# Retention attention before two feed-forward experts: attention in units of half a batch, with states packed

## The chip, the cores and the metric

One NeuronCore of a Trainium2 chip runs the whole program. The metric is device time in microseconds of one execution, a median over timed runs. In the profile, PE is TensorE's matmuls and PEld its weight loads, DVE is VectorE, ACT ScalarE, POOL GpSimd, and SP SyncE, from which all transfers are issued.

## The reference

A decayed attention without softmax feeds two feed-forward layers, all in float32:

```
q, k, v: 4 batches x 8 heads x 576 positions x 64
scores = (q @ k^T) / 8
scores *= gamma_h ** (i - j)  for i >= j, else 0     (gamma_h = 1 - 2**(-5-h))
x = scores @ v                                       -> 2304 tokens x 512
h = max(max(x @ w1, x @ w2), x @ w3)                 512 -> 768
x2 = h @ w_out                                       768 -> 512
out = (silu(x2 @ w_gate) * (x2 @ w_val)) @ w_out2    512 -> 1536 -> 512
```

## The kernel before

**The attention.** Positions are cut into chunks of 96, three chunks to a half-batch of 288 positions. Heads go in pairs, so that two heads of 64 fill 128 partitions. Within a chunk the scores are computed and masked by the decay; what earlier chunks contribute is carried in a 64 x 64 state per head. `halves` lists 32 units (batch, head pair, half), the half running fastest, so a batch is complete after eight units. `a_load` loads a whole batch's keys, queries and values of a head pair (six transfers for two units). `a_prep` transposes keys and queries of a unit on TensorE through an identity (line 149), copies the keys out on ScalarE (kt, 153) and scales the queries by the decay on VectorE (qg, 154); for a first half GpSimd scales the keys (ks, 144). `a_score` multiplies them (168), and VectorE applies the decay mask (pT, 170). `a_state` forms the products of keys and values (185), and VectorE folds them into the running state, one 64 x 64 operation for each head and chunk (191, 193). The states lie in `stz` as 128 x 128 blocks, one head in the upper left and one in the lower right, with zeros elsewhere. `a_value` multiplies states by queries (208) and values by scores (214) into one accumulator, which leaves as a high half in float32r (xh, ScalarE, 220) and the rest (xl, VectorE, 221).

**The first expert.** Weights come as float64; `conv_w` turns a block of 128 x 512 into a high and a low float32r half, with two operations on ScalarE (102, 103), three on VectorE (104 to 106), one more on ScalarE (107) and a subtraction (108), on GpSimd for the first expert's 18 blocks, on VectorE for the later ones. `f_slice` is one *slice*: one block of 128 of the 768 hidden columns, one of w1, w2, w3, one half-batch; 12 matmuls of 288 columns (258) into one of two PSUM buffers. It is evicted on ScalarE (262) for w1 and with a maximum on VectorE (264) for w2 and w3, and after w3 stored to memory (266). There are 8 x 18 = 144 slices.

**The order.** TensorE's instructions run in the order of the program text (`manual_schedule`); those of the other engines are ordered by a planner that simulates the program. The loop over units weaves the attention of unit n (values), n+1 (scores and state) and n+2 (transposes) with slices of the batch before, in four visits: transposes, slices, scores, slices, values, slices, state, slices (lines 291 to 309). Nine slices go to two units. In the first seven units the 18 blocks are converted instead. Behind the loop stand the slices of the last batch, with the conversion of the second set of weights (`c2`, into 26 buffers that take over the attention's memory) and the reloading of h (`h_split`). Then come the product with w_out (line 381) and the second expert (from line 392 on).

Of the kernel before, what the change touches and what calls it, by code (L numbers as in the profile page):

```python
# [30 lines left out]
F1 = DF1 // P  # L31
# [31 lines left out]
def retention_moe(ctx, tc, consts, q, k, v, w1, w2, w3, w_out, w_gate, w_val, w_out2, out):  # L63
    nc = tc.nc
    pe, act, dve, pool, sp = nc.tensor, nc.scalar, nc.vector, nc.gpsimd, nc.sync

    def f(ap):
        return ap.bitcast(F32)
# [18 lines left out]
    e_t = cst[:, O_E:NCONST]  # L87
# [24 lines left out]

    halves = [(b, pr, h) for b in range(B) for pr in range(NP) for h in range(2)]
    NU = len(halves)
    U = {}
    xs = {}
    stz = [att.tile([P, 2 * NC, 2, D], F32, name=f"stz{i}", tag=f"stz{i}", bufs=1) for i in range(2)]
    for t in stz:  # L120
        pool.memset(t, 0.0)

    def a_load(u):
        if u >= B * NP:
            return
        b, pr = divmod(u, NP)
        t = {}
        for nm, s in (("k", k), ("q", q), ("v", v)):
            t[nm] = att.tile([CK, 2 * NC, 2, D], F32, name=f"{nm}n", tag=f"{nm}n", bufs=3)
# [3 lines left out]
        U[u] = t  # L133

    def a_prep(n):

        if n >= NU:
            return
        b, pr, h = halves[n]
        u = U[n // 2]  # L140
        if h == 0:
            ks = att.tile([CK, 2 * NC, 2, D], F32, name="ks", tag="ks")
            sc = ks_t[:, pr].unsqueeze(1).unsqueeze(3).to_broadcast([CK, 2 * NC - 1, 2, D])
            pool.tensor_tensor(ks[:, 0:2 * NC - 1], u["k"][:, 0:2 * NC - 1], sc, ALU.mult)
            u["ks"] = ks
        tp = psa.tile([P, 2, 512], F32, name="tp", tag="tp")
        for x, nm in ((0, "k"), (1, "q")):
            for c in range(NC):
                pe.transpose(tp[:, x, c * CK:(c + 1) * CK],  # L149
                             u[nm][:, h * NC + c].rearrange("p h d -> p (h d)"), ident)  # L150
        kt = att.tile([P, C], F32, name="kt", tag="kt")
        qg = att.tile([P, NC, CK], F32, name="qg", tag="qg", bufs=3)
        act.activation(kt, tp[:, 0, 0:C], ACTF.Copy)
        dve.tensor_tensor(qg, tp[:, 1, 0:C].rearrange("p (c m) -> p c m", c=NC),
                          g_t[:, pr].unsqueeze(1).to_broadcast([P, NC, CK]), ALU.mult)
        u[h] = {"kt": kt, "qg": qg}

    def a_score(n):
        if n >= NU:
            return  # L160
        b, pr, h = halves[n]
        w = U[n // 2][h]
        s = psa.tile([CK, 2, 512], F32, name="s", tag="s")
        for c in range(NC):
            cs = slice(c * CK, (c + 1) * CK)
            for e in range(2):
                hd = slice(64 * e, 64 * e + 64)
                pe.matmul(s[:, e, cs], w["kt"][hd, cs], w["qg"][hd, c], start=True, stop=True)  # L168
# [3 lines left out]
        w["pT"] = pT  # L172

    def a_state(n):
        if n >= NU:
            return
        b, pr, h = halves[n]
        u = U[n // 2]
        st = stz[(n // 2) % 2]
        m = psa.tile([P, NC, D], F32, name="m_ps", tag="m_ps")  # L180
        cs = [c for c in range(NC) if h * NC + c < 2 * NC - 1]
        for c in cs:
            g = h * NC + c
            for e in range(2):
                pe.matmul(m[64 * e:64 * e + 64, c], u["ks"][:, g, e], u["v"][:, g, e], start=True, stop=True)  # L185
        for c in cs:
            g = h * NC + c
            for e in range(2):
                hd = slice(64 * e, 64 * e + 64)
                if g == 0:  # L190
                    dve.tensor_copy(st[hd, 1, e], m[hd, c])
                else:
                    dve.scalar_tensor_tensor(st[hd, g + 1, e], st[hd, g, e], e_t[hd, pr:pr + 1], m[hd, c],  # L193
                                             ALU.mult, ALU.add)

    def a_value(n):
        if n >= NU or n < 0:
            return
        b, pr, h = halves[n]
        u = U[n // 2]  # L200
        w = u[h]
        st = stz[(n // 2) % 2]
        o = psa.tile([P, C], F32, name="o_ps", tag="o_ps")
        first = True
        for c in range(NC):
            g = h * NC + c
            if g:
                pe.matmul(o[:, c * CK:(c + 1) * CK], st[:, g].rearrange("p e d -> p (e d)"), w["qg"][:, c],  # L208
                          start=first, stop=False, skip_group_check=True)
                first = False  # L210
        for c in range(NC):
            g = h * NC + c
            for e in range(2):
                pe.matmul(o[64 * e:64 * e + 64, c * CK:(c + 1) * CK], u["v"][:, g, e], w["pT"][:, e, c],  # L214
                          start=False, stop=True, skip_group_check=True)
        if h == 0:
            u["x"] = [ffn.tile([P, S], F32R, name=f"x{x}", tag=f"x{x}{pr}", bufs=2) for x in "hl"]
        xh, xl = u["x"]
        ts = slice(h * C, h * C + C)
        act.activation(xh[:, ts], o, ACTF.Copy)  # L220
        dve.tensor_tensor(xl[:, ts], o, f(xh[:, ts]), ALU.subtract)
        xs[(2 * b + h, pr)] = (xh[:, ts], xl[:, ts])
        if h == 1:
            U.pop(n // 2)
# [52 lines left out]
    a_load(0)  # L277
    win_load(0)
    a_load(1)
    win_load(1)  # L280
# [8 lines left out]
    a_load(2)  # L289
    a_score(0)  # L290
    for n in range(NU):
        if n % 8 == 0 and n:
            b = n // 8 - 1
            fq += [(2 * b + h, fi, wi) for fi in range(F1) for wi in range(3) for h in range(2)]
        if n % 2 == 0:
            a_load(n // 2 + 3)
        quota = (2, 1, 1, 1) if n % 2 else (1, 1, 1, 1)
        ncv = (3 if n % 2 else 2) if n < 7 else 0
        a_prep(n + 2)
        f_some(quota[0])  # L300
        for _ in range(ncv):
            win_conv(wc)
            wc += 1
        a_score(n + 1)
        f_some(quota[1])
        a_value(n)
        f_some(quota[2])
        a_state(n + 1)
        f_some(quota[3])
    while wc < len(win_units):  # L310
        win_conv(wc)
        wc += 1
    f_some(99)
    pe_order.__exit__(None, None, None)
    psa_cm.__exit__(None, None, None)
    att_cm.__exit__(None, None, None)
# [157 lines left out]
```

## Time and profile before

| | us |
|---|---|
| three runs | 936.71, 936.80, 938.08; median 936.8 |
| profiled execution | 936.91 |
| its span, first to last instruction | 935.1 |
| TensorE busy (PE) | 898.9, 96% |
| VectorE busy (DVE) | 431.6, 46% |
| ScalarE busy (ACT) | 262.9, 28% |
| GpSimd busy (POOL) | 163.7, 18% |
| mean DMA rate | 71 GB/s |

The shares are means over stages of different kinds. The page's row of busy tenths shows TensorE at 9 in nearly all of 40 slices of the span, but at 5 to 8 in the first four, and VectorE at 8 or 9 in the second to fourth. The rows further down are from the single stages.

### The profile page before, as it was taken

How to read it: one execution, taken by the hardware profiler on the slowest of the kernel's cores; microseconds unless marked ns; L12 is line 12 of the kernel's file. 1: busy time of each engine (PE TensorE's matmuls, PEld its weight loads, DVE VectorE, ACT ScalarE, POOL GpSimd, SP SyncE). 2: the span in 40 equal slices, each digit the busy share in tenths (PEclk: the TensorE clock that was granted, in tenths of full speed). 3: DMA queues.
4: the chain of work that ended last, by engine and by line, in shares of the span. 5: the costliest groups of instructions: out<-in, count | busy, mean ns of one | idle time of the engine just before them, and what ended most of it. 6: DMA issues, size and time to landing. Idle time of an engine off the chain costs nothing.

```text
span 935.1 us, 14209 instructions
## 1 busy us (share of the span) xinstructions
PE 898.9 (96%) x5832; PEld 786.4 (84%) x5832; DVE 431.6 (46%) x816; ACT 262.9 (28%) x512; POOL 163.7 (18%) x148
## 2 busy tenths in 40 slices
PE   5876999999999999999999999999999999999998
PEld 4756999999999998999988888888888888888886
DVE  4899543444344388111172173465257335333243
ACT  2555111111111175034363271142133123111111
POOL 3354000000000040044411111111112111111111
PEclk9998999999999999999999999999999999999999
DMA  9975522322210166123240040021012000000112
GB/s 221 230 189 159 126 66 52 77 59 58 65 33 20 46 200 201 39 65 90 76 121 15 1 120 15 1 87 49 1 45 91 1 1 1 1 0 1 46 69 89
DMA packets 98225, 66.06 MB, mean 71 GB/s; under 512 B 59632, under 2 KB 93424, under 8 KB 98160
## 3 DMA queue, kind: packets, MB, share of 16 engines
q1 hardware_dynamic: 98160, 65.15, 25.3%
q8 instruction: 46, 0.75, 0.3%
q14 instruction: 19, 0.16, 0.0%
HBM read 53.34 MB, written 11.80 MB: 70 GB/s over the span
## 4 chain that ended last, share of the span: by engine, by line
PE 84%; DVE 7%; DMA 3%; issue 2%; ACT 2%; POOL 1%; SPq 0%; POOLq 0%; DVEq 0%; ACTq 0%
PE ps L406 31%; PE ps L258 22%; PE ps L428 15%; PE ps L381 7%; DVE wz L105 2%; PE o_ps L214 2%; PE s L168 2%; PE o_ps L208 2%; PE tp L149 1%; DVE wz L104 1%; DVE wl L106 1%; PE m_ps L185 1%; DMA h_d<-hmax 1%; DMA w<-in_moe_w_gate_dram 1%; DVE stz L193 1%
## 5 line engine op out<-in xcount | busy, mean ns | idle before, releaser
L258 PE MATMUL ps<-xl,wh 128*128 128x288 f32 x576 | 181.4, 315 | 9.6 <-DVE hmax L264 7.2
L406 PE MATMUL ps<-x2l,wrh 128*128 128x512 f32 (+1 forms) x480 | 179.3, 374 | 0.8 <-DVE sg L414 0.8
L406 PE MATMUL ps<-x2h,wrl 128*128 128x512 f32 (+1 forms) x480 | 179.1, 373 | 0.0
L406 PE MATMUL ps<-x2h,wrh 128*128 128x512 f32 (+1 forms) x480 | 179.1, 373 | 0.0
L258 PE MATMUL ps<-xh,wlo 128*128 128x288 f32 x576 | 170.8, 297 | 0.0
L258 PE MATMUL ps<-xh,wh 128*128 128x288 f32 x576 | 170.5, 296 | 0.0
L417 POOL TENSOR_TENSOR gl<-gf,gh 128x512 fp32r<-128x512 f32 (+1 forms) x60 | 75.3, 1256 | 388.7 <-ACT gh L416 388.7
L258 PEld LDWEIGHTS ps<-xl,wh 128*128 128x128 f32 x576 | 109.3, 190 | 18.8 <-DVE hmax L264 9.0
L414 DVE TENSOR_TENSOR sg<-ps,sg 128x512 f32<-128x512 f32 (+1 forms) x60 | 38.2, 636 | 171.1 <-ACT sg L413 171.1
L258 PEld LDWEIGHTS ps<-xh,wlo 128*128 128x128 f32 x576 | 109.4, 190 | 0.0
L258 PEld LDWEIGHTS ps<-xh,wh 128*128 128x128 f32 x576 | 109.2, 190 | 0.0
L406 PEld LDWEIGHTS ps<-x2l,wrh 128*128 128x128 f32 x480 | 90.4, 188 | 19.7 <-DVE sg L414 1.6
L406 PEld LDWEIGHTS ps<-x2h,wrl 128*128 128x128 f32 x480 | 90.3, 188 | 17.8
L406 PEld LDWEIGHTS ps<-x2h,wrh 128*128 128x128 f32 x480 | 90.4, 188 | 17.7
L428 PE MATMUL ps<-wrh,gl 128*128 128x512 f32 x216 | 85.8, 397 | 0.4 <-POOL gl L417 0.4
L428 PE MATMUL ps<-wrl,gh 128*128 128x512 f32 x216 | 85.5, 396 | 0.0
L428 PE MATMUL ps<-wrh,gh 128*128 128x512 f32 x216 | 85.2, 394 | 0.0
L413 ACT ACTIVATE sg<-ps 128x512 f32<-128x512 f32 (+1 forms) x60 | 33.2, 554 | 166.6 <-PE ps L406 166.6
L264 DVE TENSOR_TENSOR hmax<-ps,hmax 128x288 f32<-128x288 f32 x96 | 43.8, 456 | 76.4 <-PE ps L258 71.9
L416 ACT ACTIVATE gh<-gf 128x512 fp32r<-128x512 f32 (+1 forms) x60 | 35.2, 586 | 121.3 <-DVE gf L415 121.3
L415 DVE TENSOR_TENSOR gf<-ps,sg 128x512 f32<-128x512 f32 (+1 forms) x60 | 38.2, 637 | 65.9 <-PE ps L406 64.8
L355 POOL TENSOR_TENSOR hl<-hf,hh 128x288 fp32r<-128x288 f32 x48 | 40.4, 860 | 143.3 <-ACT hh L354 142.3
(51 smaller groups left out, 1233.6 us busy)
## 6 DMA issues: line engine op xcount, KB each, us to landing
w<-in_moe_w_dram SPq DMA_DIRECT2D x18, 512.0 KB, 4.8
w<-in_moe_w_out_dram SPq DMA_DIRECT2D x18, 512.0 KB, 3.7
h_d<-hmax SPq DMA_DIRECT2D x48, 144.0 KB, 1.8
hf<-h_d SPq DMA_DIRECT2D x48, 144.0 KB, 2.2
w<-in_moe_w_gate_dram SPq DMA_DIRECT2D x12, 512.0 KB, 4.4
w<-in_moe_w_val_dram SPq DMA_DIRECT2D x12, 512.0 KB, 4.6
kn<-in_k_dram SPq DMA_DIRECT2D x32, 144.0 KB, 4.2
qn<-in_q_dram SPq DMA_DIRECT2D x32, 144.0 KB, 4.4
```

What stands on the lines that cost most here:

```text
L105: dve.scalar_tensor_tensor(z, u[:, :, 1], 0x80000000, z, ALU.bitwise_and, ALU.bitwise_or)
L258: pe.matmul(ps, l[:, ksl], r, start=n == 0, stop=n == 3 * KD - 1)
L264: dve.tensor_tensor(mx[hb], ps, mx[hb], ALU.max)
L355: pool.tensor_tensor(hl, hf, f(hh), ALU.subtract)
L381: pe.matmul(ps, l[:, es], r, start=n == 0, stop=n == 3 * F1 - 1)
L406: pe.matmul(ps[:, 0:tw], l[:, ksl], r, start=n == 0, stop=n == 3 * KD - 1)
L413: act.activation(sg[:, 0:tw], pr[0][:, 0:tw], ACTF.Sigmoid)
L414: dve.tensor_tensor(sg[:, 0:tw], pr[0][:, 0:tw], sg[:, 0:tw], ALU.mult)
L415: dve.tensor_tensor(gf[:, 0:tw], pr[1][:, 0:tw], sg[:, 0:tw], ALU.mult)
L416: act.activation(gh[:, 0:tw], gf[:, 0:tw], ACTF.Copy)
L417: pool.tensor_tensor(gl[:, 0:tw], gf[:, 0:tw], f(gh[:, 0:tw]), ALU.subtract)
L428: pe.matmul(ps, l[:, sl], r, start=n == 0, stop=n == 3 * GRP - 1)
```

## The change

Units are now (batch, half, head pair), the pair running fastest, so that a half-batch is complete after four units. Each unit has its own loads, four units ahead. A loop pass makes one visit of values n, state n+1 and scores n+1, then slices, then the preparation of n+2, then slices. From unit 8 on (`PT`) keys and queries are loaded once more in pieces of 32 partitions with runs of 32 numbers (8 more transfers a unit, the ones for natural queries left out), and VectorE transposes them in blocks of 32 x 32. The state of both heads is one packed 128 x 64 operation; two ScalarE copies a unit spread it into zeroed tiles, and the product with the queries is made for each head with 64 columns. Conversions are due one a unit in units 1 to 3 and three a unit in 4 to 8; slices start at unit 4 with three a unit, and five a unit from unit 9 on. The last half-batch's 18 slices stand behind the loop.

```diff
-    halves = [(b, pr, h) for b in range(B) for pr in range(NP) for h in range(2)]
+    PT = 8
+    units = [(b, h, pr) for b in range(B) for h in range(2) for pr in range(NP)]
...
+            if nm == "q" and n >= PT:
+                continue
+            u[nm] = att.tile([CK, NC, 2, D], F32, name=f"{nm}n", tag=f"{nm}n", bufs=4)
             for e in range(2):
-                sp.dma_start(out=t[nm][:, :, e, :],
-                             in_=s[b, 2 * pr + e].rearrange("(a p) d -> p a d", p=CK))
+                sp.dma_start(out=u[nm][:, :, e, :],
+                             in_=s[b, 2 * pr + e, c0:c0 + C].rearrange("(a p) d -> p a d", p=CK))
+        if n >= PT:
+            u["t"] = att.tile([P, 2, C // 32, 32], F32, name="qk", tag="qk", bufs=3)
+            for i, s in enumerate((k, q)):
+                for e in range(2):
+                    for x in range(2):
+                        g = 64 * e + 32 * x
+                        sp.dma_start(out=u["t"][g:g + 32, i],
+                                     in_=s[b, 2 * pr + e, c0:c0 + C, 32 * x:32 * x + 32].rearrange("(a p) d -> p a d", p=32))
...
+            qt = att.tile([P, C], F32, name="qt", tag="qt", bufs=2)
+            dve.transpose(kt.rearrange("p (a d) -> p a d", d=32), u["t"][:, 0])
+            dve.transpose(qt.rearrange("p (a d) -> p a d", d=32), u["t"][:, 1])
+            dve.tensor_tensor(qg, qt.rearrange("p (c m) -> p c m", c=NC), g, ALU.mult)
...
+        for c in range(nk):
             g = h * NC + c
+            if g == 0:
+                act.activation(st[:, 1], m[:, c], ACTF.Copy)
+            else:
+                dve.scalar_tensor_tensor(st[:, g + 1], st[:, g], e_t[:, pr:pr + 1], m[:, c], ALU.mult, ALU.add)
+        z = stz[n % 3]
+        for e in range(2):
+            hd = slice(64 * e, 64 * e + 64)
+            act.activation(z[hd, 1 - h:NC, e], st[hd, h * NC + 1 - h:(h + 1) * NC], ACTF.Copy)
...
+                if c or h:
+                    pe.matmul(oc, z[:, c, e], u["qg"][:, c], start=c == 1 - h, stop=False, skip_group_check=True)
...
     a_prep(0)
-    win_conv(wc)
-    wc += 1
     a_state(0)
+    a_score(0)
     a_prep(1)
...
+        if n % NP == 0 and n:
+            fq += [(n // NP - 1, fi, wi) for fi in range(F1) for wi in range(3)]
+        a_load(n + 4)
+        a_value(n)
+        a_state(n + 1)
+        a_score(n + 1)
+        quota, ncv = ((2, 3) if n >= 9 else (1, 2)), 0
+        if 1 <= n < 4:
+            ncv = 1
+        elif 4 <= n < 9:
+            ncv = 3
+        for _ in range(min(ncv, len(win_units) - wc)):
             win_conv(wc)
             wc += 1
+        f_some(quota[0])
+        a_prep(n + 2)
         f_some(quota[1])
...
-    fq += [(2 * (B - 1) + h, fi, wi) for fi in range(F1) for wi in range(3) for h in range(2)]
+    fq += [(NHB - 1, fi, wi) for fi in range(F1) for wi in range(3)]
     for i in range(F1):
         c2()
         h_split(0, i)
-        f_some(6)
+        f_some(3)
     f_some(99)
```

## Rows read from the trace of the kernel before

**Rows 1.** Windows: busy us (x instructions) of each engine, clock, DMA share, GB/s.
```profile
6.50:95.50 89.00, 67.83 (x516) 57.50 (x516) 78.78 (x145) 43.72 (x82) 35.08 (x25) 0.96 0.86 203
120.00:300.00 180.00, 180.00 (x1696) 168.00 (x1693) 74.04 (x188) 25.05 (x61) 10.01 (x8) 1.00 0.21 56
```

**Rows 2.** Groups by line, VectorE, 6.5 to 95.5 us: count, busy us, mean ns, idle before.
```profile
L105 DVE SCALAR_TENSOR_TENSOR wz<-w,wz 128x512 uint32<-128x512 uint32 x20 | 20.3, 1013 | 0.5
L104 DVE TENSOR_SCALAR wz<-wz 128x512 uint32<-128x512 uint32 x21 | 16.3, 777 | 0.7 <-ACT wz L102 0.5
L106 DVE CUSTOM_DVE_ANT_0 wl<-wz,wl 128x1024 uint16<-128x1024 uint16 x20 | 15.7, 787 | 0.7
L193 DVE SCALAR_TENSOR_TENSOR stz<-stz,cst,m_ps 64x64 f32<-64x64 f32 x40 | 11.1, 278 | 1.0
L170 DVE TENSOR_TENSOR pT<-s,cst 96x576 f32<-96x576 f32 x10 | 7.5, 751 | 0.8 <-PE s L168 0.7
L154 DVE TENSOR_TENSOR qg<-tp,cst 128x288 f32<-128x288 f32 x12 | 5.5, 455 | 9.9 <-ACT kt L153 9.6
```

**Rows 3.** Chain of work that ended last: start us, us, what.
```profile
371.45 24.13 PE ps L258 x180
395.58 7.17 PE ps L381 x54
```

**Rows 4.** TensorE in order of time, 201 to 223 us: start us, us, line.
```profile
201.15 0.75 PE L168 MATMUL s<-qg,kt 64*96 64x96 f32 x12
201.84 0.40 PE L258 MATMUL ps<-xl,wh 128*128 128x288 f32 x1
...
203.53 0.80 PE L208 MATMUL o_ps<-qg,stz 128*128 128x96 f32 x6
204.27 0.72 PE L214 MATMUL o_ps<-pT,vn 96*64 96x96 f32 x12
204.91 0.40 PE L258 MATMUL ps<-xl,wh 128*128 128x288 f32 x1
...
206.69 0.57 PE L185 MATMUL m_ps<-vn,ks 96*64 96x64 f32 x12
207.19 0.40 PE L258 MATMUL ps<-xl,wh 128*128 128x288 f32 x1
...
208.89 0.41 PE L149 MATMUL tp<-cst,kn 96*128 96x96 f32 x3
...
209.33 0.38 PE L258 MATMUL ps<-xl,wh 128*128 128x288 f32 x1
...
211.09 0.75 PE L168 MATMUL s<-qg,kt 64*96 64x96 f32 x12
...
222.29 0.75 PE L168 MATMUL s<-qg,kt 64*96 64x96 f32 x12
```

**Rows 5.** TensorE in order of time, 19.5 to 26 us, one unit of the front.
```profile
19.81 0.74 PE L149 MATMUL tp<-cst,kn 96*128 96x96 f32 x3
...
20.96 1.28 PE L168 MATMUL s<-qg,kt 64*96 64x96 f32 x12
22.17 1.59 PE L208 MATMUL o_ps<-qg,stz 128*128 128x96 f32 x6
23.69 1.23 PE L214 MATMUL o_ps<-pT,vn 96*64 96x96 f32 x12
24.71 0.85 PE L185 MATMUL m_ps<-vn,ks 96*64 96x64 f32 x12
25.49 0.74 PE L149 MATMUL tp<-cst,kn 96*128 96x96 f32 x3
```

**Rows 6.** Groups by line, 329.8 to 395.4 us: the first of three matmul groups.
```profile
L258 PE MATMUL ps<-xl,wh 128*128 128x288 f32 x152 | 46.1, 303 | 2.3 <-DVE hmax L264 1.4 <-ACT hmax L262 0.7
```

**Rows 7.** Line 131's transfers, ns to issue min/median/max: 100 to 330, 0 to 40 us.
```profile
L131 SPq DMA_DIRECT2D qn<-in_q_dram x14: 457/478/501, 114.3 to 241.6; - x14
...
L131 SPq DMA_DIRECT2D vn<-in_v_dram x10: 313/780/1642, 3.3 to 39.4; - x10
```

More of the change, by code (lines that the diff above doesn't have):

```diff
@@ L111, in cols, with a_load @@
         return w[:, c0:c0 + P].rearrange("(a p) n -> p a n", p=P)
-    halves = [(b, pr, h) for b in range(B) for pr in range(NP) for h in range(2)]
-    NU = len(halves)
+    PT = 8
+    units = [(b, h, pr) for b in range(B) for h in range(2) for pr in range(NP)]
+    NU = len(units)
     U = {}
     xs = {}
-    stz = [att.tile([P, 2 * NC, 2, D], F32, name=f"stz{i}", tag=f"stz{i}", bufs=1) for i in range(2)]
+    states = {}
+    stz = [att.tile([P, NC, 2, D], F32, name=f"stz{i}", tag=f"stz{i}", bufs=1) for i in range(3)]
     for t in stz:
         pool.memset(t, 0.0)
-    def a_load(u):
-        if u >= B * NP:
+    def a_load(n):
+        if n >= NU:
             return
-        b, pr = divmod(u, NP)
-        t = {}
+        b, h, pr = units[n]
+        c0 = h * C
+        u = {}
         for nm, s in (("k", k), ("q", q), ("v", v)):
-            t[nm] = att.tile([CK, 2 * NC, 2, D], F32, name=f"{nm}n", tag=f"{nm}n", bufs=3)
+            if nm == "q" and n >= PT:
+                continue
+            u[nm] = att.tile([CK, NC, 2, D], F32, name=f"{nm}n", tag=f"{nm}n", bufs=4)
             for e in range(2):
-                sp.dma_start(out=t[nm][:, :, e, :],
-                             in_=s[b, 2 * pr + e].rearrange("(a p) d -> p a d", p=CK))
-        U[u] = t
+                sp.dma_start(out=u[nm][:, :, e, :],
[8 more added lines that the diff above has]
+                                     in_=s[b, 2 * pr + e, c0:c0 + C, 32 * x:32 * x + 32].rearrange("(a p) d -> p a d", p=32))
+        U[n] = u
     def a_prep(n):
@@ L138, in a_prep @@
             return
[L139 to L150, printed above, removed]
@@ L151, in a_prep @@
-        kt = att.tile([P, C], F32, name="kt", tag="kt")
-        qg = att.tile([P, NC, CK], F32, name="qg", tag="qg", bufs=3)
[L153 to L156, printed above, removed]
+        b, h, pr = units[n]
+        u = U[n]
+        nk = NC - h
+        u["ks"] = att.tile([CK, NC, 2, D], F32, name="ks", tag="ks", bufs=3)
@@ new lines, in a_prep @@
+        sc = ks_t[:, pr].unsqueeze(1).unsqueeze(3).to_broadcast([CK, nk, 2, D])
+        pool.tensor_tensor(u["ks"][:, 0:nk], u["k"][:, 0:nk], sc, ALU.mult)
+        kt = att.tile([P, C], F32, name="kt", tag="kt", bufs=2)
+        qg = att.tile([P, NC, CK], F32, name="qg", tag="qg", bufs=3)
+        g = g_t[:, pr].unsqueeze(1).to_broadcast([P, NC, CK])
+        if n < PT:
+            tp = psa.tile([P, 2, 512], F32, name="tp", tag="tp")
+            for x, nm in ((0, "k"), (1, "q")):
+                for c in range(NC):
+                    pe.transpose(tp[:, x, c * CK:(c + 1) * CK],
+                                 u[nm][:, c].rearrange("p h d -> p (h d)"), ident)
+            act.activation(kt, tp[:, 0, 0:C], ACTF.Copy)
+            dve.tensor_tensor(qg, tp[:, 1, 0:C].rearrange("p (c m) -> p c m", c=NC), g, ALU.mult)
+        else:
[3 more added lines that the diff above has]
+            dve.tensor_tensor(qg, qt.rearrange("p (c m) -> p c m", c=NC), g, ALU.mult)
@@ L160, in a_score @@
             return
-        b, pr, h = halves[n]
-        w = U[n // 2][h]
+        b, h, pr = units[n]
+        u = U[n]
         s = psa.tile([CK, 2, 512], F32, name="s", tag="s")
@@ L167, in a_score @@
                 hd = slice(64 * e, 64 * e + 64)
-                pe.matmul(s[:, e, cs], w["kt"][hd, cs], w["qg"][hd, c], start=True, stop=True)
+                pe.matmul(s[:, e, cs], u["kt"][hd, cs], u["qg"][hd, c], start=True, stop=True)
         pT = att.tile([CK, 2, NC, CK], F32, name="pT", tag="pT")
@@ L176, in a_state @@
             return
-        b, pr, h = halves[n]
-        u = U[n // 2]
-        st = stz[(n // 2) % 2]
+        b, h, pr = units[n]
+        u = U[n]
+        nk = NC - h
         m = psa.tile([P, NC, D], F32, name="m_ps", tag="m_ps")
-        cs = [c for c in range(NC) if h * NC + c < 2 * NC - 1]
-        for c in cs:
-            g = h * NC + c
+        for c in range(nk):
+            for e in range(2):
+                pe.matmul(m[64 * e:64 * e + 64, c], u["ks"][:, c, e], u["v"][:, c, e], start=True, stop=True)
@@ new lines, in a_state @@
+        if h == 0:
+            st = states[(b, pr)] = att.tile([P, 2 * NC, D], F32, name="st", tag=f"st{pr}")
+        else:
+            st = states.pop((b, pr))
+        for c in range(nk):
+            g = h * NC + c
+            if g == 0:
+                act.activation(st[:, 1], m[:, c], ACTF.Copy)
+            else:
+                dve.scalar_tensor_tensor(st[:, g + 1], st[:, g], e_t[:, pr:pr + 1], m[:, c], ALU.mult, ALU.add)
+        z = stz[n % 3]
+        for e in range(2):
+            hd = slice(64 * e, 64 * e + 64)
+            act.activation(z[hd, 1 - h:NC, e], st[hd, h * NC + 1 - h:(h + 1) * NC], ACTF.Copy)
@@ L184, in a_state, with a_value @@
+    def a_value(n):
+        b, h, pr = units[n]
+        u = U.pop(n)
+        z = stz[n % 3]
+        o = psa.tile([P, C], F32, name="o_ps", tag="o_ps")
+        for c in range(NC):
             for e in range(2):
-                pe.matmul(m[64 * e:64 * e + 64, c], u["ks"][:, g, e], u["v"][:, g, e], start=True, stop=True)
-        for c in cs:
-            g = h * NC + c
+                oc = o[64 * e:64 * e + 64, c * CK:(c + 1) * CK]
+                if c or h:
+                    pe.matmul(oc, z[:, c, e], u["qg"][:, c], start=c == 1 - h, stop=False, skip_group_check=True)
+        for c in range(NC):
@@ L188, in a_state @@
             for e in range(2):
[L189 to L214, printed above, removed]
-                          start=False, stop=True, skip_group_check=True)
[L216 to L224, printed above, removed]
@@ L227, in retention_moe @@
+                pe.matmul(o[64 * e:64 * e + 64, c * CK:(c + 1) * CK], u["v"][:, c, e], u["pT"][:, e, c],
+                          start=False, stop=True, skip_group_check=True)
+        xh, xl = [ffn.tile([P, C], F32R, name=f"x{x}", tag=f"x{x}{pr}", bufs=3) for x in "hl"]
+        act.activation(xh, o, ACTF.Copy)
+        dve.tensor_tensor(xl, o, f(xh), ALU.subtract)
+        xs[(2 * b + h, pr)] = (xh, xl)
     w_in = {}
@@ L277, in retention_moe @@
     a_load(0)
+    a_load(1)
     win_load(0)
-    a_load(1)
-    win_load(1)
+    a_load(2)
+    a_load(3)
     wc = 0
```

24 lines of the change are left out of this document (2 added, 22 removed).

## The prediction

> **What bounds the kernel now.** I read the windows by stage first, then the groups by line in the front, then TensorE's instructions in order of time. Up to 95.5 us VectorE sets the pace: it is busy 78.8 of 89.0 us (88.5%) while TensorE has gaps [rows 1]. What fills it is the conversion of the first expert's 18 weight blocks, 1.01 + 0.78 + 0.79 = 2.58 us of VectorE each, beside the attention's own operations [rows 2]. From 120 to 300 us TensorE is busy 180 of 180 us and VectorE 74 [rows 1]: there only TensorE's own work counts. The chain shows 15 slices in a row (180 matmuls, 12 a slice) in 24.13 us, 1.61 us a slice, and the second product (line 381) begins at 395.58 us [rows 3]. All after that point is untouched by the diff, so the sum is for the time of that point. The profiled execution took 936.91 us (span 935.1 and 1.8 around it), the median of the three timed runs is 936.8: no correction.
>
> **One unit in the steady part, before.** From score to score the first unit takes 211.09 - 201.15 = 9.94 us with four slices, the next 222.29 - 211.09 = 11.20 with five [rows 4]. Nine slices at 1.60 are 14.4, so attention costs (21.14 - 14.4)/2 = 3.37 us a unit. Inside the first unit the attention's own instructions are score 0.69, states times queries 0.74, values 0.64, state 0.50, transposes 0.44: 3.01. The rest, 9.94 - 6.40 - 3.01 = 0.53, is what four visits cost in starting and ending among slices: 0.13 each.
>
> **One unit after, from unit 9 on** (no transposes on TensorE, one visit, five slices behind it). Values 0.64, score 0.69, state 0.50 stay. The states' product was six matmuls of 128 columns; it becomes four or six of 64 columns for each half, in pairs on the two column halves. The trace has no such matmul with 128 rows. The nearest is the value product, whose halves lie on the column halves too: 12 in 0.64, 0.053 each [rows 4]. At that pace four to six are 0.21 to 0.32, mean 0.27. The other bound is that the pair doesn't overlap: 0.74/6 = 0.123 each, mean 0.62. I take 0.27, since the 96-row pairs differ only in rows. For entering and leaving I take 0.25: one visit is 0.13, and the visit now holds one more change of shape, from state to score.
> The trace can be counted in two ways here. By visits it is 0.13; the Trainium skill, "TensorEngine Tiling (Array Packing)", Key Properties, says that a change of tiling mode (not of tile) drains TensorE. Before, a unit has six such changes (into and out of scores, values and state; 0.53/6 = 0.09), after it three (slices to values, state to scores, scores to slices), 0.27 by that count. By the one the sum is 3 us lower than with 0.25, by the other 0.5 us higher.
> So a unit's attention is 0.64 + 0.69 + 0.50 + 0.27 + 0.25 = 2.35 us instead of 3.37, and its period with five slices 10.35 us.
>
> **The front.** Half-batches now come complete after four units instead of after eight units (a whole batch), so slices start at unit 4. TensorE's early pace is slower: the same score takes 22.17 - 20.96 = 1.21 us, values 1.02, state 0.78, transposes 1.15 [rows 5], against 0.69, 0.64, 0.50, 0.44 later, although the granted clock of the whole stretch is 0.96 in the mean [rows 1]. With 0.7 for the states' product a unit takes 4.9 us there. The first loads are half as large; I put the start of unit 0's values at 10 us, and unit 4 at 10 + 4 x 4.9 = 30 us. Until then only three conversions are due.
> From unit 4 to 8 three conversions are due per unit and VectorE binds again. Its work until all 18 blocks are converted: conversions 18 x 2.58 = 46.4; queries 11 x 0.455 = 5.0; scores 10 x 0.751 = 7.5; low halves of the output 9 x 0.455 = 4.1; states 20 x 0.278 = 5.6 (one operation on 128 x 64 for two on 64 x 64, of the same length by my choice, and the first of a first half goes to ScalarE); slices 10 x 0.455 = 4.5; six new transposes 2.7: 75.8 us [rows 2]. From 7 us on, at the 88.5% of before, that ends at 93. But unit 9's slices need only the first 15 blocks and then three more in turn: 3 x 2.58/0.885 = 8.7 us less, 84, and I take 86 for the start of unit 9 (by units: three conversions 7.7, attention 2.4 and slices 0.9 are 11.0 of VectorE's time a unit, and five of them from 30 on end at 85).
>
> **From unit 9 to line 381.** 15 of 144 slices are done. In the loop 111 remain: 177.6 us. Attention 23 x 2.35 less the missing last state and score, 52.9. Behind the loop 18 slices, 28.8. Before, the last 38 slices took 65.6 us against 60.8 at 1.60; the 4.8 are waits for evictions behind the next conversions [rows 6], which are all still there: I keep 4.8. Sum 264: line 381 starts at 350, 45 us earlier.
>
> **What I cost at nothing.** *VectorE in the steady part*: the new 32 x 32 transposes of 128 x 288 are not in the trace. I take 0.455 (same shape from PSUM); below nothing isn't possible, since they replace no VectorE work, and above I take 1.01 (the slowest 512-column row). A unit's VectorE work is then 3 x 0.455 + 0.751 + 0.455 + 0.56 + 1.5 = 4.6, at most 5.7, of 10.35 us. If this cover fails, an eviction waits behind the two transposes and the scaling (1.4, at most 2.5 us) and TensorE with it, having two accumulators: rival 2. *ScalarE* gains two small copies a unit and has 25 of 180 us in use [rows 1]; their path, state to copy to next visit, has five slices (8 us) of room. *POOL*: the same scaling of keys in smaller pieces. *SyncE and DMA*: a unit from 8 on issues 12 loads where two units shared 6, and its keys are loaded twice. At 0.478 us an issue [rows 7] that is 5.7, with 5/3 stores 6.4 of 10.35 us. Runs of 128 bytes double the pieces per unit; if each costs what one of 256 does, the DMA share of 0.21 [rows 1] becomes 0.4. Loads are four units ahead. The 18 blocks' loads are the same ones. *After the last values* 21 slices (34 us) cover the first six second-set conversions, which line 381 needs, as 38 did before.
>
> **Rivals.**
> 1. *Slow pace between 30 and 86 us.* TensorE has gaps there, and the same instructions are 1.75 times as long in the front (1.21/0.69). A unit would be 3 x 2.8 + 4.9 (3.75 from unit 6 on) = about 12.6 instead of 11.2: +7, end 899. For it: the granted clock of the stretch up to 95.5 us is 0.96 in the mean, so it fell to its lower level, 1.2 GHz, for a while [rows 1]. Against: slices come each few us.
> 2. *Evictions late in the steady part.* VectorE's work lies in one bunch around one visit, and a hmax eviction has 1.6 us. At 0.6 us a unit: +14, end 905; at 1.0, 914. For it: rows 6 show just such waits when VectorE is full. Against: it is full at 45% only.
> 3. *The unit doesn't shrink as said*: 64-column pairs one after another (+0.35) and shape changes dearer (+0.2): 23 x 0.55 = 13, end 904.
> 4. *Slower: SyncE's issue.* The loads of units 8 and on become the bound. Early loads took up to 1.64 us to issue, with a median of 0.78 [rows 7]. At 1.05 each a unit takes 12 x 1.05 + 0.6 = 13.2 us; 23 units are 304, plus 33.6 behind them and 86: line 381 at 423, end 965. It is slower than before from (395.6 - 86 - 33.6)/23 = 12.0 us a unit, 0.95 an issue. For it: the loads' halved runs and twice the issues. Against: 0.48 an issue where DMA isn't full. The Trainium skill, "DMA: Bandwidth & Descriptors", Specifications, wants transfers of 512 bytes for line rate, which speaks for this rival; no row here shows runs of 128.
> 5. *Better*: conversions pulled into the idle front, unit 9 at 76: end 881.
>
> **How the numbers follow.** Forecast 936.9 - 45.3 = 891.6, 891. Chances: forecast 0.45 (own range 884 to 898), rival 1 0.14, 2 0.17, 3 0.08, 4 0.05, 5 0.10, no change in sum 0.01. The range is 873 to 913: below, rival 5 with visits at 0.13 (878) and without the 4.8 of the last slices; above, rival 2 at its 914. Within 0.2%, 1.9 us, is about what a measurement can tell from no change: 0.01; faster 0.94, slower 0.05.
>
> **What would show it.** In the changed profile: slices from about 33 us; 15 done near 86; periods of 10.3 us with one visit; 12 values 0.64 and states' pairs 0.27; no gap of TensorE over 0.2 us between 100 and 310 us; line 381 near 350, and from there to the end of the span 539.5 us as before. It is wrong if TensorE waits for qk loads or for hmax in the steady part, or if unit 9 starts after 100 us.

## The result, and the profile after

The changed kernel takes 902.64 us (median of 4 runs, 902.10 to 904.41), the kernel before 936.75 on the same chip: ratio 0.9641, 95% interval 0.9619 to 0.9662. The forecast was 891 with 873 to 913: the direction and the range hold, and 11 us of the forecast gain did not come. The profiled execution took 902.46 us, 900.7 of them span.

Windows of the changed kernel by stage (busy us and instructions of TensorE, its weight loads, VectorE, ScalarE, POOL; granted clock; DMA share; GB/s). The first and the fourth answer to [rows 1]:

```profile
6.50:95.50 89.00, 66.61 (x648) 60.05 (x649) 66.37 (x125) 47.15 (x102) 34.44 (x31) 0.83 0.84 191
10.53:40.98 30.45, 19.38 (x197) 16.70 (x196) 16.29 (x33) 12.61 (x31) 10.00 (x10) 0.73 0.80 185
40.98:95.37 54.39, 43.23 (x417) 40.15 (x417) 48.28 (x88) 33.29 (x68) 23.34 (x19) 0.87 0.86 195
120.00:300.00 180.00, 180.00 (x1848) 174.14 (x1848) 76.11 (x183) 33.25 (x92) 12.06 (x17) 1.00 0.35 76
24.30:51.60 27.30, 18.00 (x152) 16.03 (x153) 19.23 (x36) 14.19 (x30) 8.83 (x8) 0.50 0.84 190
```

The second row is units 0 to 3. VectorE, which was busy 88.5% of the whole front before, has work for 16.3 of 30.5 us there, and TensorE for 19.4: no engine is the bound, and TensorE is idle for 11.1 us. The third row is units 4 to 8: VectorE 88.8%. The fourth is the steady part, TensorE without a pause.

TensorE of the changed kernel in order of time, one visit of the steady part, the counterpart of [rows 4], and the first instruction of the second product, the counterpart of [rows 3]:

```profile
202.41 0.29 PE L269 MATMUL ps<-xh,wh 128*128 128x288 f32 x1
202.64 0.55 PE L227 MATMUL o_ps<-qg,stz 128*64 128x96 f32 x8
203.02 0.67 PE L230 MATMUL o_ps<-pT,vn 96*64 96x96 f32 x12
203.52 0.40 PE L202 MATMUL m_ps<-vn,ks 96*64 96x64 f32 x8
203.85 0.75 PE L186 MATMUL s<-qg,kt 64*96 64x96 f32 x12
204.53 0.40 PE L269 MATMUL ps<-xl,wh 128*128 128x288 f32 x1
204.77 0.29 PE L269 MATMUL ps<-xh,wlo 128*128 128x288 f32 x1
...
359.26 0.30 PE L385 MATMUL ps<-hl,wrh 128*128 128x288 f32 x1
```

The line numbers have moved: slices 258 to 269, second product 381 to 385, and so on. From one start to the next the states' product takes 0.38 (0.55 where there are 12 records in place of 8), the values 0.50, the state 0.33 (or 0.45), the scores 0.68. Line 385 starts at 359.3, where 350 was forecast, and 541.4 us follow it, 539.5 before.

The starts of the units' value visits tell where the 11 us were lost (TensorE in order of time, us; the forecast's row is worked out from its terms, unit 31 with 98 slices after unit 11's):

| unit | 0 | 1 | 2 | 3 | 4 | 9 | 10 | 11 | 31 | line 385 |
|---|---|---|---|---|---|---|---|---|---|---|
| forecast | 10 | 14.9 | 19.8 | 24.7 | 30 | 86 | 96.4 | 106.7 | 310.5 | 350 |
| measured | 10.5 | 17.0 | 21.4 | 33.4 | 41.0 | 95.4 | 109.2 | 121.4 | 321.4 | 359.3 |

The loss arises in two places: units 2 and 3 (11 us late by unit 4), and units 9 and 10 (13.8 and 12.2 us for a period of 10.3, 5.3 us in all). What happens in unit 2 is seen with all engines in one order of time:

```profile
20.69 0.47 SPq L93 DMA_DIRECT2D w<-in_moe_w_dram  x1
21.44 0.55 PE L227 MATMUL o_ps<-qg,stz 128*64 128x96 f32 x8
24.79 0.66 ACT L102 ACTIVATE wz<-w 128x512 f32<-128x512 f32 x1 [3.89 <-DMA w<-in_moe_w_dram]
25.47 0.43 DVE L104 TENSOR_SCALAR wz<-wz 128x512 uint32<-128x512 uint32 x1 [5.00 <-ACT wz L102]
25.81 0.75 DVE L188 TENSOR_TENSOR pT<-s,cst 96x576 f32<-96x576 f32 x1
25.90 0.40 ACT L167 ACTIVATE kt<-tp 128x288 f32<-128x288 f32 x1
26.61 0.91 PE L230 MATMUL o_ps<-pT,vn 96*64 96x96 f32 x8 [4.62 <-DVE pT L188]
```

Read from below: TensorE waits 4.62 us for the masked scores `pT`. VectorE had their input, but the operation ahead of it in its queue was a step of a weight's conversion (line 104), which waited 5.00 us for ScalarE's step (line 102), and this waited 3.89 us for a transfer that SyncE had issued only at 20.69: 34 loads of keys, queries and values of units 0 to 5 stood ahead of it, and SyncE had issued one transfer every 0.55 us from 0.73 on. The copy `kt` stood behind line 102 in ScalarE's queue in the same way. Neither engine was at work: an operation that waits for a transfer blocked those behind it. Two more such waits follow, ahead of units 3 and 4:

```profile
33.36 1.23 PE L227 MATMUL o_ps<-qg,stz 128*64 128x96 f32 x8 [2.52 <-ACT stz L216]
39.21 0.48 DVE L172 STREAM_TRANSPOSE qt<-qk 128x288 f32<-128x288 f32 x1 [2.65 <-DMA qk<-in_q_dram]
40.98 1.44 PE L227 MATMUL o_ps<-qg,stz 128*64 128x96 f32 x11 [1.84 <-ACT stz L216]
```

At 33.36 TensorE waits for the states' copy (line 216), which stood behind a conversion that waited 1.40 us for its weight. At 40.98 it waits for the same copy of the next unit; that one waited for VectorE, whose head of queue was the transpose of a small load of queries. So the small loads already held up the front here, beside the weights.

At 24.3, while TensorE waited, its granted clock fell to 0.50 (1.2 GHz), and it stayed there until 51.6. Before 20.9 TensorE ran at the slower pace too: the clock column gives 1.00 there (for 10.5 to 20.9 us), but the scores take 1.28 us each, as they do under 0.50 and not as under 1.00:

```profile
14.60 1.28 PE L186 MATMUL s<-qg,kt 64*96 64x96 f32 x12 [1.56 <-DVE qg L168]
28.41 1.28 PE L186 MATMUL s<-qg,kt 64*96 64x96 f32 x12
58.96 0.75 PE L186 MATMUL s<-qg,kt 64*96 64x96 f32 x12
```

So 0.73 and 0.83 in the windows above are too high; the length of the scores tells the level.

The second place, all engines again, at units 9 and 10:

```profile
99.07 0.67 ACT L102 ACTIVATE wz<-w 128x512 f32<-128x512 f32 x1 [4.05 <-DMA w<-in_moe_w_out_dram]
102.16 0.41 ACT L273 ACTIVATE hmax<-ps 128x288 f32<-128x288 f32 x1
102.62 0.45 PE L269 MATMUL ps<-xl,wh 128*128 128x288 f32 x1 [1.81 <-ACT hmax L273]
...
107.57 0.67 ACT L102 ACTIVATE wz<-w 128x512 f32<-128x512 f32 x1 [5.00 <-DMA w<-in_moe_w_out_dram]
108.70 0.40 ACT L273 ACTIVATE hmax<-ps 128x288 f32<-128x288 f32 x1
```

The same figure, with a slice's eviction (`hmax`) in the place of `pT`, and with weights of the second set, which are wanted only by the product at line 385, after 350 us. The planner had put their conversions this early.

### The profile page after: what moved, and what is told of

Same layout as the page of the kernel before. It is cut to its first block, busy times and chain, and to the rows that moved or that the text cites. A ratio compares the mean times of both kernels' runs of the same rounds, so it can differ in the third digit from the quotient of the medians.

```text
span 900.7 us, 14609 instructions
## 1 busy us (share of the span) xinstructions
PE 859.2 (95%) x5848; PEld 759.0 (84%) x5848; DVE 412.3 (46%) x768; ACT 276.1 (31%) x568; POOL 165.9 (18%) x165
## 4 chain that ended last, share of the span: by engine, by line
PE 79%; DMA 11%; ACT 3%; DVE 2%; SPq 2%; issue 2%; POOL 1%; POOLq 0%; DVEq 0%; ACTq 0%
PE ps L410 33%; PE ps L269 19%; PE ps L432 16%; PE ps L385 6%; DMA w<-in_moe_w_dram 4%; PE s L186 2%; DMA w<-in_moe_w_gate_dram 2%; DMA hf<-h_d 1%; DMA w<-in_moe_w_out_dram 1%; SPq L136 1%; PE o_ps L227 1%; PE o_ps L230 1%; DMA kn<-in_k_dram 1%; DMA vn<-in_v_dram 1%; PE m_ps L202 1%
## 5 line engine op out<-in xcount | busy, mean ns | idle before, releaser
L269 PE MATMUL ps<-xl,wh 128*128 128x288 f32 x576 | 175.6, 305 | 12.9 <-ACT hmax L273 10.7
L269 PEld LDWEIGHTS ps<-xl,wh 128*128 128x128 f32 x576 | 110.0, 191 | 18.1 <-ACT hmax L273 12.3
L275 DVE TENSOR_TENSOR hmax<-ps,hmax 128x288 f32<-128x288 f32 x96 | 43.5, 454 | 106.4 <-PE ps L269 91.5
L420 ACT ACTIVATE gh<-gf 128x512 fp32r<-128x512 f32 (+1 forms) x60 | 35.2, 586 | 121.4 <-DVE gf L419 121.4
L438 DVE TENSOR_TENSOR acc<-ps,acc 128x512 f32<-128x512 f32 x90 | 61.9, 690 | 3.2 <-PE ps L432 2.7
```

The costliest lines, as they stand in the source:

```text
L269: pe.matmul(ps, l[:, ksl], r, start=n == 0, stop=n == 3 * KD - 1)
L275: dve.tensor_tensor(mx[hb], ps, mx[hb], ALU.max)
L420: act.activation(gh[:, 0:tw], gf[:, 0:tw], ACTF.Copy)
L438: dve.tensor_tensor(a, ps, a, ALU.add)
```

## The experiments

The theory after the result, A: the first expert's weights land too late, and what waits for them holds up the front. Rivals: TensorE's lower clock (C); the keys' and queries' small loads (S); the conversions pulled in from the second set (P). Four more runs are on the steady part. In the edits, "..." marks what is left out.

**Weights early** (`w_early`): loads three ahead, in five buffers of their own, the first three between the units' loads.

```diff
...
-        win_load(i + 1)
+        for j in range(i + 1, i + 4):
+            win_load(j)
...
```

> Same work; the weight blocks of the first expert are loaded into five buffers of their own, three blocks ahead, and the first three stand between the first units' loads. Theory A (a weight block comes late because its load stands behind the many small loads of SyncE's queue, and the conversions that wait for it stand ahead of the attention's operations on ScalarE and VectorE): ScalarE's waits for weights before 30 us go, unit 4's values start at about 33 us (41.0 in the changed kernel), unit 9's at 84 to 89 (95.4), line 385 at 348 to 353 (359.3), time 892 to 897. Rival B (TensorE's lower clock from 24 to 51 us sets the front): unit 9 stays within 2 us of 95, time 901 to 905. Rival C (VectorE's amount of work sets it, as predicted): the same, 901 to 905.

Measured 901.86 us, ratio 0.9624 (0.9608 to 0.964): no difference from 0.9641 that the intervals allow to claim. Unit 4 came at 37.7 and unit 9 at 91.5, 3 to 4 us earlier, but unit 10 only at 109.4: 18 us for one unit, with TensorE waiting 4.2 us for an eviction at 101.7. The gain at the first place was given back at the second. How large it was is not certain: `three_calls` below, whose program is that of the change up to unit 9, had unit 4 at 38.3 and unit 9 at 93.5. Nor are the waits gone: at 28.0 ScalarE waited 3.65 us for a weight, and from 8 to 122 us it waited 8.5 us for the first set's weights (18.2 with the change) and 5.5 for the second's (10.9).

**Clock** (`warm`): twelve multiplications of zeros in each of units 0 to 4.

```diff
...
+        if n < 5:
+            warm(12)
```

> Same result; adds 12 matmuls of zeros, 128 x 128 on 288 columns, behind the scores in each of units 0 to 4, so that TensorE has dense work there. Rival B: the clock rises before 20 us and stays, unit 4's values start at 36 us or earlier, unit 9's at 89 or earlier, time 893 to 898. Theory A: the granted clock may be full, but unit 4's values stay within 2 us of 41.0 and unit 9's of 95.4, since the waits are for weights; time 900 to 905.

Measured 898.59 us, ratio 0.9578 (0.9563 to 0.9594), 4 us faster than the change. Its scores in units 2 to 4, and its window over the second stretch:

```profile
21.96 0.75 PE L186 MATMUL s<-qg,kt 64*96 64x96 f32 x12
29.99 1.28 PE L186 MATMUL s<-qg,kt 64*96 64x96 f32 x12 [1.28 <-DVE qg L168]
36.33 0.75 PE L186 MATMUL s<-qg,kt 64*96 64x96 f32 x12
```
```profile
41.00:95.40 54.40, 45.33 (x452) 42.40 (x453) 51.13 (x90) 33.16 (x67) 24.62 (x19) 0.91 0.86 202
```

By the scores TensorE was at its upper level at 22 and 36 us and at the lower one at 30, where the change has the lower one from 24.3 to 51.6; the granted clock of the second stretch is 0.91 in place of 0.87. Unit 4 starts at 39.3, unit 9 at 90.8. But ScalarE's and VectorE's operations also came out in another order here, so whether the 4 us are the clock's is not shown.

**All the front's transposes on TensorE** (`pt16`): the small loads begin with unit 16.

```diff
-    PT = 8
+    PT = 16
```

> TensorE transposes units 8 to 15 too, so the small loads of units 8 to 15 (64 issues, six more queries' loads in their place per two units) are gone from the front. Units 8 to 15 then cost TensorE 0.44 for transposes and 0.13 for one more visit, 4.6 us in all. Theory A: unit 9's values start at 88 to 92 (95.4), line 385 at 355 to 360, time 898 to 903. Rival B: unit 9 at 95, time 906 to 909. Rival C: six transposes (3 us) less on VectorE, unit 9 at 92, time 903 to 906.

Measured 899.72 us, ratio 0.9598 (0.9581 to 0.9616). Unit 9 starts at 95.4 as with the change, but units 9 and 10 take 10.7 us each, where 13.8 and 12.2 had been. They contain 0.5 us of transposes more and are still shorter: the second place stalls no more. Two things are gone from it: the small loads, and the second set's conversions, of which the planner put none between 96 and 119 us here (four begin there with the change). The run doesn't separate them.

**Slices late** (`late`): slices wait for whole batches, from unit 8 on.

```diff
...
-        if n % NP == 0 and n:
-            fq += [(n // NP - 1, fi, wi) for fi in range(F1) for wi in range(3)]
+        if n % 8 == 0 and n:
+            fq += [(n // NP - 2 + i, fi, wi) for i in range(2) ...]
...
```

> Slices start only when a whole batch is complete (unit 8, as in the kernel before), everything else as changed; one more buffer for the outputs of a head pair. If TensorE's time before unit 9 is idle time, the 15 slices of units 4 to 8 move behind it whole: line 385 later by 15 x 1.6 = 24 us less what unit 9 comes earlier for (up to 8 us), time 918 to 927. If the conversions set the front and the slices cost it nothing either way: as late by 24. If slices so early were worth nothing: 903.

Measured 923.07 us, ratio 0.9845 (0.9816 to 0.9874); line 385 starts at 384.0 in a profiled execution of 925.88. Without the early slices 20 of the 34 us are gone. The 14 that are left hold the gain of the shorter unit and the losses of the front together, so they do not price the shorter unit. By the periods, 10.57 in the mean with four and a half slices of 1.60 before [rows 4] and 10.18 with five after, a unit's attention is 1.2 us shorter, an estimate of 27 us in 23 units.

**No second-set conversions in the attention** (`no_pull`): their staging buffers lie in memory that comes free with the attention's.

```diff
...
-        z = stg.tile([P, 512], U32, name="wz", tag="wz", bufs=2)
+        z = stgs[-1].tile([P, 512], U32, name="wz", tag="wz", bufs=2)
...
```

> Same work; the staging buffers of the second set of weights come from memory that is free only behind the attention's last unit, so none of its conversions can stand among units 9 and 10. Theory D (ScalarE waits there for w_out at the head of its queue, 4.05 and 5.0 us, and the slices' evictions stand behind it): units 9 and 10 take 10.2 us each (13.8 and 12.2 in the changed kernel), no gap of TensorE over 0.5 us between 96 and 320 us, line 385 at 353 to 355 (359.3) if the last 21 slices still take 37 us, time 896 to 899. Rival: the gaps are VectorE's left-over work or the dip of the clock: units 9 and 10 stay above 12 us, time 901 to 904. Rival: what is gained there is lost behind the loop, where the conversions start later: the last 21 slices and line 385's stage take 5 us more, time 901 to 904.

Measured 902.66 us, ratio 0.9637 (0.9623 to 0.9652). It is the only edit of the front that left ScalarE's order as it was up to unit 9. Units 9 and 10 take 12.3 and 10.1 us, not 10.2 each: in unit 9 a small load now stands in the conversions' place at the head of VectorE's queue, with an eviction behind it, for which TensorE waits 1.86 us.

```profile
104.60 0.48 DVE L173 STREAM_TRANSPOSE qt<-qk 128x288 f32<-128x288 f32 x1 [4.34 <-DMA qk<-in_q_dram]
```

Unit 11 starts at 119.1 in place of 121.4; behind the loop the conversions that had been early are missing, and 40.2 us pass from the last visit to line 385 in place of 37.9. P moves 2.3 us from one place to another.

**No weight transfers** (`no_wload`): 17 of the first set's 18 loads are left out.

```diff
...
+            win_ld[i] = win_ld0[0] if win_ld0 else load_w(...)
...
```

> Leaves out 17 of the 18 loads of the first expert's weights: all 18 conversions read the first block, so that none waits for a transfer. Theory A: unit 4's values start at 30 to 35 us (41.0), unit 9's at 84 to 88 (95.4), as the sum with VectorE's work says; line 385 at 347 to 354. Rival B (the lower clock of TensorE): unit 4 at 38 or later. Rival C (VectorE has more work than summed): unit 4 early, but unit 9 at 93 or later.

Measured 901.54 us (two executions). The window of the time that units 0 to 3 take with the change:

```profile
10.50:41.00 30.50, 18.52 (x179) 15.70 (x178) 26.93 (x43) 20.38 (x44) 16.29 (x13) 1.00 0.52 110
```

After the one block's load none of the first set's weights is waited for, and the time is the same. The conversions now fill VectorE (26.9 of 30.5 us) ahead of the attention's operations: units 1 to 4 start at 20.8, 29.5, 38.3 and 45.9, later than with the transfers, and unit 9 at 100.2. So A falls as the sole cause, though this run is no clean test either: the planner drew the conversions forward, three of them ahead of unit 1's state copy (one with the change). Whether the conversions wait or work, they stand ahead of the small operations that TensorE's fixed order needs next.

**Early weights and no second set** (`early_no_pull`): both edits from above.

> Same work; the early weight loads and the barred second-set conversions together. If both waits are what is left of the front, unit 9's values start at 91 or earlier and units 9 and 10 take 10.2 us each: line 385 at 349 to 352, time 893 to 896. If the gain of either is lost to the other's queue as it was with the early loads alone: 898 to 902.

Measured 902.11 us, ratio 0.9632 (0.9609 to 0.9656). A window, two scores on TensorE, a wait of ScalarE, then VectorE in order of time:

```profile
10.50:41.00 30.50, 23.07 (x223) 19.67 (x225) 21.25 (x39) 15.47 (x37) 11.62 (x12) 1.00 0.83 183
```
```profile
41.62 1.28 PE L187 MATMUL s<-qg,kt 64*96 64x96 f32 x12
56.46 0.75 PE L187 MATMUL s<-qg,kt 64*96 64x96 f32 x12
```
```profile
28.83 0.66 ACT L103 ACTIVATE wz<-w 128x512 f32<-128x512 f32 x1 [4.83 <-DMA w<-in_moe_w_dram]
```
```profile
94.14 0.48 DVE L173 STREAM_TRANSPOSE qt<-qk 128x288 f32<-128x288 f32 x1 [2.52 <-DMA qk<-in_q_dram]
100.03 0.48 DVE L173 STREAM_TRANSPOSE qt<-qk 128x288 f32<-128x288 f32 x1 [3.77 <-DMA qk<-in_q_dram]
```

Nothing is gained, though unit 9 starts at 93.3. The 1.00 of the window is no full clock: the scores take 1.28 us up to 41.62, so TensorE ran at the slower pace there as with the change, and this run says nothing against C. The waits for the second set's weights are gone, but 11.7 us of waits for the first set's are left. Later VectorE waits at the head of its queue for the small loads of q, evictions behind it, and unit 9 takes 15 us.

**The small loads from GpSimd's queue** (`qk_pool`).

```diff
-                        sp.dma_start(out=u["t"][g:g + 32, i],
+                        pool.dma_start(out=u["t"][g:g + 32, i],
```

> The eight small loads of k and q of a unit (from unit 8 on) are issued from GpSimd's queue in place of SyncE's; nothing else changes. Theory S, that SyncE's issuing holds up the weights and the k and q loads in the front: SyncE has about 4 us less to issue for each unit from 4 on (the loads run four units ahead), the conversions end by 88 in place of 95, unit 9 starts by 91 in place of 95.4, line 385 at 355, the time about 898. Rival Q, that the order of the in-order queues of ScalarE and VectorE makes the waits whichever queue issues: unit 9 at 94 to 97 and the time within 2 us of 902.6. If GpSimd's own work (the scaling of k) is pushed behind its issuing, states wait for it, and the steady period rises above 10.3.

Measured 906.53 us, ratio 0.9676 (0.9655 to 0.9696). Both expectations miss, and why is plain in the order of time of all engines at the start:

```profile
13.78 0.66 ACT L102 ACTIVATE wz<-w 128x512 f32<-128x512 f32 x1 [5.12 <-DMA w<-in_moe_w_dram]
...
23.13 0.66 ACT L102 ACTIVATE wz<-w 128x512 f32<-128x512 f32 x1 [5.01 <-DMA w<-in_moe_w_dram]
...
24.25 0.22 ACT L210 ACTIVATE st<-m_ps 128x64 f32<-128x64 f32 x1
...
25.63 1.23 PE L227 MATMUL o_ps<-qg,stz 128*64 128x96 f32 x8 [10.08 <-ACT stz L216]
```

The planner, given other queues, put two conversions ahead of unit 0's state copy; each waited 5 us for its transfer, and unit 0 began at 25.6 in place of 10.5. From there on, however, the front ran faster: 99.7 us from unit 0 to unit 11 (110.9 with the change), the last two units 10.2 and 10.1. Of those 11.2 us part is the head start that the conversions had, so S is not priced by this run.

**Other order in the visit** (`swap`): values, scores, state; one change of shape more.

```diff
         a_value(n)
-        a_state(n + 1)
         a_score(n + 1)
+        a_state(n + 1)
```

> Same work; in the one visit the order is values, scores, state instead of values, state, scores. If a visit costs by its start and end alone, the steady period of a unit stays 10.15 us. If each change of tile shape costs 0.09, there is one more (values to scores, scores to state, state to slices) and the period is 10.24, line 385 2 us later.

Measured 911.82 us in one execution only, so the trace counts here more than the time. The visit, TensorE in order of time:

```profile
209.61 0.67 PE L230 MATMUL o_ps<-pT,vn 96*64 96x96 f32 x12
210.21 0.75 PE L186 MATMUL s<-qg,kt 64*96 64x96 f32 x12
210.89 0.45 PE L202 MATMUL m_ps<-vn,ks 96*64 96x64 f32 x8
```

The values last 0.60 where they are followed by the scores, 0.50 where the state follows in the same shape. The steady period is 0.15 longer in the mean (202.9 us from unit 11 to 31 for 200.0), some 3 us in all. The other 6 are the front's, whose queues came out in another order again (unit 9 at 102.2).

**Visits split up** (`three_calls`): from unit 9 on a slice between the stages, and two fewer behind them.

```diff
         a_value(n)
+        if n >= 9:
+            f_some(1)
         a_state(n + 1)
+        if n >= 9:
+            f_some(1)
         a_score(n + 1)
...
```

> From unit 9 on the three stages of a unit no longer stand together: one slice is put between values and states and one between states and scores, so that a unit has five stretches of attention and slices in place of three; the work is the same. Theory: in the steady part TensorE is what bounds, and each time it goes from the slices' shape to attention's and back costs about 0.13 us. Two more such visits a unit, 22 units: the period rises from 10.15 to about 10.4 us and the time by about 6 us, to 908. Rival: the change of shape costs nothing by itself, and the gain of the steady part came from packing alone: the period stays within 0.05 us of 10.15 and the time at 902 to 903.

Measured 913.86 us, ratio 0.9748 (0.9728 to 0.9768); the period is 10.6 to 10.9 us (units 11 to 31 in 211.3 us for 200.0). TensorE in order of time around a state that stands alone:

```profile
219.10 0.29 PE L269 MATMUL ps<-xh,wh 128*128 128x288 f32 x1
219.33 0.45 PE L202 MATMUL m_ps<-vn,ks 96*64 96x64 f32 x8
219.71 0.40 PE L269 MATMUL ps<-xl,wh 128*128 128x288 f32 x1
219.95 0.29 PE L269 MATMUL ps<-xh,wlo 128*128 128x288 f32 x1
```

The last slice matmul before the visit keeps TensorE 0.23 in place of 0.13, the state 0.38 in place of 0.33, the first slice matmul after it 0.24 in place of 0.13: 0.25 us a visit, twice what I had expected. I had taken the 0.13 of the prediction for the whole; the rest of it is inside the stages' own durations. With the values 0.10 longer where a slice follows them, two visits are 0.55 us a unit, 11 us in all.

**All transposes on TensorE** (`pt32`).

```diff
-    PT = 8
+    PT = 32
```

> All 32 units' transposes on TensorE, as units 0 to 7 have them; no loads of k and q in the transposed layout, no transposes on VectorE. Theory: the steady part goes at TensorE's pace, so the six transposes of a unit and the visit around them cost their full length there, about 0.5 us a unit as units 9 to 14 showed when the first 16 units had them so (10.6 to 10.7 in place of 10.15). The run with 16 took 899.7, 16 more units add 8 us: 908. Rival: the transposes on VectorE and their eight small loads a unit cost as much elsewhere (SyncE's issuing, VectorE's queue) as they save on TensorE: 899 to 902, no later than the run with 16.

Measured 907.59 us, ratio 0.9682 (0.9665 to 0.97), as the theory had it (908). The periods are 10.5 to 10.9 us. TensorE in order of time in the middle of one:

```profile
206.30 0.41 PE L165 MATMUL tp<-cst,kn 96*128 96x96 f32 x3
206.54 0.41 PE L165 MATMUL tp<-cst,qn 96*128 96x96 f32 x3
```

In the steady part VectorE's transposes hide (0.46 and 0.48 us each, VectorE at 76 of 180 us) and take 0.5 us a unit off TensorE: units 15 to 31 last 167.5 us here and 159.6 with `pt16`.

**Three of them together** (`pt16_early_warm`).

> Three changes together that each took 0.7 to 4 us alone: the first 16 units' transposes on TensorE, the first expert's weights loaded three ahead in buffers of their own, and twelve multiplications of zeros in units 0 to 4 that keep TensorE's granted clock up. If each takes away a different part of the front's delay, the gains add: 0.7 + 4.0 + 2.9 less, about 895. If they all shorten the same stretch, of which one is enough, the time is that of the best of them alone, 898 to 899; line 385 then starts at 356 to 357, as with the zeros alone.

Measured 892.87 us, ratio 0.9521 (0.9503 to 0.9539): 9.8 us better than the change by the medians, where the three alone add up to 7.7; by the ratios it is 11.2 for 11.5, so the gains add as far as can be told. It beats both kernels. Windows, and the first instruction of the second product (line 385 is 398 in this kernel):

```profile
10.50:41.00 30.50, 24.14 (x284) 21.92 (x282) 22.94 (x43) 17.42 (x43) 12.52 (x13) 0.94 1.00 222
41.00:95.40 54.40, 47.67 (x497) 44.78 (x498) 50.47 (x87) 33.67 (x73) 24.46 (x19) 0.97 0.91 219
```
```profile
350.98 0.29 PE L398 MATMUL ps<-hl,wrh 128*128 128x288 f32 x1
```

Unit 9 starts at 88.4 and unit 11 at 109.7. VectorE is busy 22.9 and 50.5 us in the two stretches in place of 16.3 and 48.3: the front's idle time is what was won. ScalarE's waits for weights from 8 to 122 us fall from 29.1 us to 3.7, and the scores take 0.75 from 23.7 on, so waits and clock both changed; which won how much is not shown. The second product starts at 351.0, a microsecond from the forecast of the change itself.

## Why the prediction was right or wrong

*Direction and range: right.* The two sources named are the real ones. Early slices are worth 20 us (`late`); of the shorter unit, two of the three visits saved are worth 11 (`three_calls`) and the transposes on VectorE some 8 between units 16 and 31 (`pt32` against `pt16`).

*The steady unit: right, its terms less so, and in part by luck.* Period 10.0 to 10.3, in the mean 10.18, for 10.35. The states' product was under-sized (0.46 in the mean for 0.27): the sum counted four to six matmuls at 0.053, but that pace had been taken over the records of both halves, of which there are 8 to 12 (0.42 to 0.64 at 0.053). Against it the values (0.50 for 0.64) and the state (0.39 for 0.50) were over-sized, so the errors nearly cancel: their old durations held part of the change of shape that goes with each visit. By visits I had counted 0.13; it is 0.25. Counting by changes was the better way to see what goes: the Trainium skill, "TensorEngine Tiling (Array Packing)", Key Properties, has a change of tiling mode drain TensorE; `swap`, with one more, agrees in sign and measures 0.15 us for it, the estimate from [rows 4] was 0.09. `three_calls`, with three more by the same count, gives 0.19 each. The stretch from unit 11 to 31 took 200.0 us, 3.8 less than its 98 slices at 1.60 and 20 visits at 2.35.

*What was costed at nothing: right in the steady part.* From 117 to 320 us TensorE has no gap over 0.2 us; VectorE's transposes took 0.46 to 0.48 us (0.455 taken). DMA share 0.35 for 0.4. Rivals 2 and 4 did not happen there.

*The front: wrong, and this is the step that failed:* "unit 4 at 10 + 4 x 4.9 = 30 us". It came at 41.0. The sum took TensorE's busy time as the pace, because VectorE had work for only three conversions, and put the waits at nothing. The busy time was right: 19.4 us for 4 x 4.9 = 19.6. What was missing are 11.1 us of TensorE's waits. Units 0 and 1 kept the pace (6.4 and 4.5 us). In units 2 and 3 (11.9 and 7.6) VectorE was busy 10.7 and ScalarE 7.8 of 20 us, and idle at the head of their queues: they waited for weights and once for a small load, with the attention's operations behind. The stretch after it, VectorE-bound at 11 us a unit, was right: 54.4 us for units 4 to 8, 10.9 each, at 88.8%. A second piece of the same kind, 5.3 us, fell on units 9 and 10, where the sum had no wait at all.

*Rival 1, the slow pace,* was partly true: by clock and scores the lower level held up to 51.6 us but for 20.9 to 24.3. It held longer before the change too: there the scores take 1.28 us up to 63.4 and 0.75 from 74.4, so the mean of 0.96 in [rows 1], from which the rival took a lower clock for a while, says too much. The 4.9 us a unit were measured at the lower level, so the clock does not explain the 11.1 us of waits up to unit 4. What it cost from unit 4 on is open: with it kept up by zeros 4 us came back, in another order of the queues.

*Behind the loop:* 21 slices took 36.7 us, 33.4 at the steady pace and 3.3 over it (4.8 taken). From line 385 on 541.4 us for 539.5.

The books: 14.7 us late at unit 11, 3.8 back in the steady part, 1.6 back behind it, 1.9 lost after line 385: 11.2 us late. The profiled execution is 10.9 above the 891.6; the 0.3 between is rounding and the time around the span.

What stays open is the price of each wait in the front. Every edit of the front but `no_pull` also changed the order in which the planner put ScalarE's and VectorE's operations, so the single runs don't isolate weights, clock and small loads. Shown is that taking away one of them, in whole or in part, moved the time by about 4 us at most; that in `no_pull`, the one with the order unchanged up to unit 9, the next one waited in its place; and that three together gave 9.8 us.

## What to carry to other kernels

Where engines work their queues in order, a stage with no busy engine can still be slow: look what stands at the head of each queue, what it waits for, and what is behind it. An operation that waits for a transfer is no filler for an idle engine ahead of that transfer's landing; take away one such wait and look for the next before pricing the gain. On TensorE count the changes of shape, in and out, with the neighbours' lengthened instructions, not the gaps alone.

## What the runs showed of the hardware

A short visit of another shape among slices costs 0.25 us here, spread over three instructions of which each looks normal by itself. SyncE's issue of the small loads took 0.45 us each in the median, more than the 0.41 of the first set's 512 KB weight loads; their 36 KB landed 2.1 us after the issue in the median, 3.0 (queries) and 4.7 (keys) between 20 and 100 us. The clock column of the profile's windows gives 1.00 in the first stretch of these runs while the scores take 1.28 us for 0.75: the length of a known instruction shows the level there.
